# One kernel at its two ends: the order and norms of the first batch's scores, its first folds in single blocks, and the last short tile with its stores

## The chip, the cores and the metric

The kernel runs on one core of one Trainium2 chip. The metric is device time in microseconds (us) of one execution. The profile was taken from one execution of its own. Its engines are PE (TensorE), ACT (ScalarE), DVE (VectorE), POOL (GpSimd) and SP (SyncE); the latter two and ACT also issue DMA transfers.

## The reference

Four batches of 5824 tokens with 256 channels pass through an attention across channels, and the 23296 tokens that come out through a feed-forward part:

```python
qn = q / (np.linalg.norm(q, axis=1, keepdims=True) + 1e-06)
kn = k / (np.linalg.norm(k, axis=1, keepdims=True) + 1e-06)
s = kn.transpose(0, 2, 1) @ qn / tau          # 256 x 256 for each batch
s = s - s.max(-1, keepdims=True)
a = np.exp(s)
a /= a.sum(-1, keepdims=True) + 1e-09
x = (v @ a).reshape(B * S, D)
out = ((x @ w1) * (x @ w2) @ w3) @ w_out      # d_ff = 1024
```

The norms run over the tokens, so that each channel of q and of k has one. tau is 1.

## The kernel before

**What is folded.** The kernel never forms v @ a. For each batch it multiplies the softmax matrix into w1 and w2 (a *fold*; the result `Wf` has 256 rows and two times 1024 columns), and w3 into w_out once (`W_sb`, 1024 x 256). Each token then needs two products with `Wf` (a and b), their elementwise product, and one product with `W_sb`.

**Tiling.** A batch has 45 groups of 128 tokens (NT) and 64 more (LEFT). A token's row lies at partition p, slot i, so that partition p owns 45 neighbouring tokens; slots come in pieces of 8, the sixth piece having five, and its slot 5 (LAST) holds the 64 left rows with zeros below them. The feed-forward part takes chunks of four slots (512 tokens) and d_ff in eight blocks of 128. The 45th slot of a batch makes a *short* tile of 128 tokens, and with it, in every second batch, go the left rows of two batches, 2 x 64 = 128 tokens. For each chunk and block PE makes a and b in one PSUM bank each (`normal`, L979), ACT casts a to bf16 (L969), DVE multiplies (L1001), and later PE makes the output tile (`emit_out` L1111; others at L1073, and L814 in a form with seven products instead of eight, whose sums POOL makes). A planner with costs and due times orders this steady part, and the scores of later batches are put between its steps.

**The head.** Only the first batch's scores are laid out by hand, at L1205 to L1253. POOL issues the loads with a cast to bf16 (`load_part` L128): k and q by pieces, last k's piece 5, the rest of q's piece 4 (slots 4 and 5, then 6 and 7), q's piece 5 (left rows, slots 0 to 2, slots 3 and 4), then v and the weights. PE makes for every slot `products` (L287: q-transposed times k into the tile G, two matmuls of 256 columns) and `squares` (L275: a slot times itself into `sqq` or `sqk`, two matmuls of 128 columns, of which only the diagonal is wanted). Between these calls stand the steps of `soft_units(0)`, in the order of the program:

- `k_first` (L302): diagonal of k's squares, on DVE.
- `k_row` (L361): one fp32 matmul of PE, then four `root_step`s (L321: Ln, Exp of half, Ln of it plus 1e-6, Exp of minus) on ACT, which give 1/(norm + 1e-6), and DVE's transpose of it into the row `kr`.
- `q_first` (L380): DVE takes the diagonal of q's squares, in two halves `dq`, with the sum `ss`.
- `scaled_first` (L310): DVE makes s = G x kr in two halves (`scale`, L396); `q_norm` (L383) makes r = 1/(norm + 1e-6) with two ACT steps and two DVE steps; ACT makes e = exp(r x s) in two halves (`exps`, L401).
- `sum_start` (L405), then fillers: two 512-column matmuls on zeros (`busy(2)`), and the transposes of v's first four slots.
- `first_folds` (L510): for each half of e, PE's row sums (L421) and `narrow_fold(0, 128)`: columns 0 to 127 of w1 and of w2 side by side in one PSUM bank for each of the two channel halves c1. DVE takes the reciprocal of the sums (L429), and the evictions to `Wf` scale by it, c1 = 0 on ACT (L506), c1 = 1 on DVE (L508). Then the same for columns 128 to 255.

The first a of the steady part needs all of columns 0 to 127 of `Wf` for w1, and the first b those for w2.

**Buffers.** PSUM has eight banks, used by tag: ab0 to ab3, out0 to out2 and G. `bank("ab")` and `bank("out")` hand out the next of their tags in turn.

**The tail.** The last chunk of 512 tokens has its output in out0 and out1; ACT evicts the former (L1143), DVE the latter (L1144), and SP stores both. The last short tile (b = 3) has its 128 tokens in out0 and the left rows of batches 2 and 3 in out2. PE makes these 16 matmuls at the very end, beginning with one of the left rows and then one of the short tile. DVE evicts the left rows (L1126), ACT the short tile (L1137). SP stores the 64 rows of batch 2 (L1129), ACT's queue the short tile (L1139) and then the 64 rows of batch 3 (L1129). After batch 1 SP makes both stores of left rows.

Of the kernel before, what the change touches and what calls it, by code (L numbers as in the profile page):

```python
# [9 lines left out]
AF = mybir.ActivationFunctionType  # L10
ALU = mybir.AluOpType
F32 = DT.float32
BF16 = DT.bfloat16

P = 128
# [15 lines left out]
def kernel(  # L31
# [12 lines left out]
    nc = tc.nc  # L44
# [35 lines left out]
    def bank(tag):  # L80

        turns[tag] += 1
        return {"tag": f"{tag}{turns[tag] % (4 if tag == 'ab' else 3)}", "bufs": 1}
# [152 lines left out]
    def busy(k):  # L236

        m = psum.tile([P, 512], F32, name=f"warm_{nc.get_next_instruction_name()}", **bank("ab"))
        for _ in range(k):
            nc.tensor.matmul(m, lhsT=warm[:, :P], rhs=warm, start=True, stop=True, skip_group_check=True)  # L240
# [26 lines left out]
    def squares(nm, pi, slots, end=False):  # L267

        if nm not in S:
            S[nm] = psum.tile([P, CT, P], F32, name=f"sq{nm}_0", **bank("out"))  # L270
        t = pieces[nm, 0, pi]
        for i in slots:
            for ct in range(CT):
                cs = slice(ct * P, (ct + 1) * P)
                nc.tensor.matmul(  # L275
                    S[nm][:, ct, :], lhsT=t[:, i, cs], rhs=t[:, i, cs],
                    start=((pi, i) == ((4, half) if nm == "k" else (0, 0)) and ct == 0),
                    stop=(end and i == slots[-1] and ct == CT - 1), skip_group_check=True,
                )

    def products(pi, slots, end=False):
        if 0 not in G_tiles:
            G_tiles[0] = psum.tile([P, CT, C], F32, tag="G", name="G_0", bufs=1)
        qt, kt = pieces["q", 0, pi], pieces["k", 0, pi]
        for i in slots:
            for ct in range(CT):
                nc.tensor.matmul(  # L287
                    G_tiles[0][:, ct, :], lhsT=qt[:, i, ct * P : (ct + 1) * P], rhs=kt[:, i, :],
                    start=(pi == 0 and i == 0 and ct == 0),
                    stop=(end and i == slots[-1] and ct == CT - 1), skip_group_check=True,  # L290
                )

    def soft_units(n):
# [14 lines left out]
            nc.vector.tensor_add(st["ksq"], red[:, :8], st["kk"])  # L308

        def scaled_first():  # L310
            for ct in range(CT):
                scale(ct)
            q_norm(st["ss"])
            exps(0)
            exps(1)

        def partition_sums(dst, src):

            nc.vector.tensor_reduce(out=dst, in_=src, axis=mybir.AxisListType.X, op=ALU.add, apply_transpose=True)

        def root_step(t, i):  # L321

            nc.scalar.activation(
                out=t, in_=t, func=(AF.Ln, AF.Exp)[i % 2],
                scale=(1.0, 0.5, 1.0, -1.0)[i], bias=eps_t if i == 2 else 0.0,
            )

# [54 lines left out]

        def q_norm(src):  # L383
            r = work.tile([P, CT], F32, tag="r", name=f"r_{n}", bufs=2)
            nc.scalar.activation(out=r, in_=src, func=AF.Ln)
            nc.scalar.activation(out=r, in_=r, func=AF.Exp, scale=0.5)
            nc.vector.tensor_scalar_add(r, r, 1e-6)
            nc.vector.reciprocal(r, r)
            if inv_tau != 1.0:
                nc.vector.tensor_scalar_mul(r, r, inv_tau)  # L390
            st["r"] = r

        def scale(ct):
# [4 lines left out]
        def exps(ct):  # L398
            if ct == 0:
                st["e"] = work.tile([P, CT, C], BF16, tag="e", name=f"e_{n}", bufs=2)  # L400
            nc.scalar.activation(  # L401
                out=st["e"][:, ct, :], in_=st["s"][:, ct, :], func=AF.Exp, scale=st["r"][:, ct : ct + 1]
            )
# [88 lines left out]
        def narrow_fold(lo, hi, c1, c2):  # L492

            if c2 == 0:
                tag = "ab" if lo < 256 else "out"
                st[lo, c1] = psum.tile([P, 2, hi - lo], F32, name=f"narrow_{lo}_{c1}", **bank(tag))
            m = st[lo, c1]
            for w in range(2):
                nc.tensor.matmul(
                    m[:, w, :], lhsT=st["e"][:, c2, c1 * P : (c1 + 1) * P], rhs=w12[:, c2, w, lo:hi],  # L500
                    start=(c2 == 0 and w == 0), stop=(c2 == CT - 1 and w == 1), skip_group_check=True,
                )
            if c2 == CT - 1:
                dst = Wf[n][:, c1, :, lo:hi]
                if c1 == 0:
                    nc.scalar.activation(out=dst, in_=m, func=AF.Copy, scale=st["rs"][:, c1 : c1 + 1])  # L506
                else:
                    nc.vector.tensor_scalar_mul(dst, m, st["rs"][:, c1 : c1 + 1])  # L508

        def first_folds():  # L510
            for c2 in range(CT):
                sum_mm(c2)
                for c1 in range(CT):
                    narrow_fold(0, P, c1, c2)
            for c1 in range(CT):
                for c2 in range(CT):
                    narrow_fold(P, 2 * P, c1, c2)
# [169 lines left out]
        agenda.append((t, seq[0], cost, fn))  # L687

    out_tiles = {}
    last_rows = []  # L690
    lefts = {}

    def chunk_cols(c):
# [398 lines left out]
    def emit_out(b, c, j, ab, only=None):  # L1092

        small = c == NCH - 1
        if small:
            lhs = [ab[:, :P]]
            if b % 2 == 1:
                lhs.append(lefts[b // 2][:, j, :, :].rearrange("p b t -> p (b t)")[:, P : P + 2 * LEFT])
        else:
            lhs = [ab[:, i // 2, i % 2 * P : (i % 2 + 1) * P] for i in range(4)]  # L1100
        if j == 0:
            out_tiles[b, c] = [
                psum.tile([P, 2, D], F32, tag=tag, name=f"o_{b}_{c}_{tag}", bufs=1)
                for tag in ((("out0", "out2") if b == B - 1 else ("out0", "out1"))[: len(lhs)] if small else ("out0", "out1"))
            ]
        tl = out_tiles[b, c]
        for s, lhsT in reversed(list(enumerate(lhs))) if small and b == B - 1 else enumerate(lhs):
            if only is not None and s != only:
                continue
            h, o = (s, 0) if small else divmod(s, 2)  # L1110
            nc.tensor.matmul(  # L1111
                tl[h][:, o, :], lhsT=lhsT, rhs=W_sb[:, j, :],
                start=(j == 0 and o == 0), stop=(j == FT - 1 and (small or o == 1)),
                skip_group_check=True,
            )
        work_on("PE", len(lhs) * (D * MM_COL + MM_FIX))
        if j == FT - 1:
            read = now["PE"] + LATE["PE"]
            free["out0"] = work_on("ACT", 0.475, read)
            free["out1"] = work_on("DVE", 0.6, read)  # L1120
            o = work.tile([P, 4, D], F32, tag="o_sb", name=f"osb_{b}_{c}", bufs=3)
            rows = out[b * N : b * N + NT * P, :].rearrange("(p i) c -> p i c", i=NT)
            if small:
                if b % 2 == 1 and only != 0:
                    o2 = work.tile([P, D], F32, tag="kr", name=f"oleft_{b}", bufs=1)
                    nc.vector.tensor_copy(o2, tl[1][:, 0, :])  # L1126
                    for m in (b - 1, b):
                        k = (m - b + 1) * LEFT
                        store = lambda m=m, k=k, queue=nc.sync: queue.dma_start(  # L1129
                            out=out[m * N + NT * P : (m + 1) * N, :], in_=o2[k : k + LEFT, :]  # L1130
                        )
                        if m < B - 1:
                            store()
                        else:
                            last_rows.append(store)
                if only != 1:
                    nc.scalar.copy(o[:, 0, :], tl[0][:, 0, :])  # L1137
                    other = nc.scalar if b == B - 1 else nc.sync
                    other.dma_start(out=rows[:, NT - 1, :], in_=o[:, 0, :])  # L1139
                    if last_rows:  # L1140
                        last_rows.pop()(queue=nc.scalar)
            else:
                nc.scalar.copy(o[:, 0:2, :], tl[0])  # L1143
                nc.vector.tensor_copy(o[:, 2:4, :], tl[1])  # L1144
                nc.sync.dma_start(out=rows[:, 4 * c : 4 * c + 4, :], in_=o)
            if only is None:
                del out_tiles[b, c]
# [86 lines left out]
    squares("k", 4, hi)  # L1234
    squares("q", 4, lo)
    products(4, lo)
    squares("k", 5, range(LAST + 1), end=True)
    soft0[0]()
    for sl in (range(half, half + 2), range(half + 2, PIECE)):
        squares("q", 4, sl)  # L1240
        products(4, sl)
    soft0[1]()
    for sl in ([LAST, 0], [1, 2]):
        squares("q", 5, sl)
        products(5, sl)
    squares("q", 5, [3, 4], end=True)
    soft0[2]()
    products(5, [3, 4], end=True)
    soft0[3]()
    soft0[6]()  # L1250
    busy(2)
    transpose_half_on_pe(0, 0, 0, False)
    soft0[4]()  # L1253

# [234 lines left out]
```

## Time and profile before

| what | value |
|---|---|
| times of three runs | 552.27, 552.76, 553.76 us; median 552.76 |
| profiled execution | 552.28 us, of which the span 550.5 us |
| busy in the span | PE 539.2 us (98%), DVE 422.6 (77%), POOL 404.9 (74%), ACT 395.6 (72%) |
| TensorE clock granted | 1.00 |
| shares of the chain that ended last | PE 93%, DMA 5%, all others under 1% |

A line such as `L401 ACT e<-s,r` is a group of instructions made at line 401, on ACT, that write tile e from s and r. The *chain of waits* is followed back from the last instruction, at each step to what released it or to the one before it on its engine. *Waits* are idle times of an engine, put down to what ended them. In a *timeline* the first column is the start in the span, the second the length, and square brackets hold the idle time before and its releaser. *Landing* is the time from the issue of a DMA to its last byte.

### The profile page before, as it was taken

How to read it: one execution, taken by the hardware profiler on the slowest of the kernel's cores; microseconds unless marked ns; L12 is line 12 of the kernel's file. 1: busy time of each engine (PE TensorE's matmuls, PEld its weight loads, DVE VectorE, ACT ScalarE, POOL GpSimd, SP SyncE). 2: the span in 40 equal slices, each digit the busy share in tenths (PEclk: the TensorE clock that was granted, in tenths of full speed). 3: DMA queues.
4: the chain of work that ended last, by engine and by line, in shares of the span. 5: the costliest groups of instructions: out<-in, count | busy, mean ns of one | idle time of the engine just before them, and what ended most of it. 6: DMA issues, size and time to landing. Idle time of an engine off the chain costs nothing.

```text
span 550.5 us, 12142 instructions
## 1 busy us (share of the span) xinstructions
PE 539.2 (98%) x4563; PEld 350.9 (64%) x4563; DVE 422.6 (77%) x742; ACT 395.6 (72%) x813; POOL 404.9 (74%) x332
## 2 busy tenths in 40 slices
PE   7799999999999999999999999999999999999996
PEld 4564566666677666666658666666657656666675
DVE  5567749999876888888766788888777787878861
ACT  5446648889777888888666888888777767677662
POOL 4170398479899399799987598969998746889360
PEclk9999999999999999999999999999999999999999
DMA  9999987986685748975683857776661334750113
GB/s 214 212 204 208 210 168 163 208 166 129 130 187 113 187 88 165 181 167 110 136 162 110 168 120 153 160 144 109 144 128 78 84 86 109 151 95 39 78 44 129
DMA packets 75018, 77.58 MB, mean 141 GB/s; under 512 B 54224, under 2 KB 58832, under 8 KB 74960
## 3 DMA queue, kind: packets, MB, share of 16 engines
q0 software_dynamic: 15664, 38.93, 40.7%
q1 hardware_dynamic: 58928, 37.17, 24.7%
q10 hardware_dynamic: 368, 0.72, 0.4%
q8 instruction: 35, 0.57, 0.4%
q14 instruction: 23, 0.19, 0.1%
HBM read 78.91 MB, written 23.86 MB: 187 GB/s over the span
## 4 chain that ended last, share of the span: by engine, by line
PE 93%; DMA 5%; ACT 0%; POOL 0%; issue 0%; DVE 0%; ACTq 0%; POOLq 0%
PE a L979 26%; PE b L979 26%; PE prodA L814 12%; PE prodC L814 6%; PE G L214 5%; PE o L1073 4%; PE X L964 3%; PE prodB L814 3%; DMA k<-in_k_dram 3%; PE fold L450 2%; DMA q<-in_q_dram 2%; PE o_out L1111 2%; PE w L1258 1%; PE Z L964 1%; PE T L964 1%; PE Y L964 1%
## 5 line engine op out<-in xcount | busy, mean ns | idle before, releaser
L1001 DVE TENSOR_TENSOR abh<-as,b 128x512 bf16<-128x512 bf16 x314 | 214.0, 684 | 74.7 <-ACT as L969 53.6
L969 ACT CAST as<-a 128x512 bf16<-128x512 f32 (+1 forms) x346 | 194.4, 563 | 67.4 <-PE a L979 53.6
L979 PE MATMUL a<-vT,Wf 128*128 128x512 bf16 x628 | 186.8, 379 | 0.1
L979 PE MATMUL b<-vT,Wf 128*128 128x512 bf16 x628 | 186.8, 379 | 0.0
L979 PEld LDWEIGHTS <-Wf 128*128 128x128 bf16 x1384 | 124.9, 98 | 80.7 <-issue 0.3
L774 POOL TENSOR_TENSOR S<-abh,abh 128x1024 bf16<-128x1024 bf16 x37 | 78.8, 2130 | 62.5 <-DVE abh L1001 52.8
L228 DVE TENSOR_TENSOR acc<-acc,sq 128x512 f32<-128x512 f32 x132 | 91.6, 694 | 1.7 <-ACT sq L211 0.8
L814 PEld LDWEIGHTS <-S 128*128 128x128 bf16 x1184 | 77.8, 98 | 22.2 <-POOL S L776 0.5
L776 POOL TENSOR_TENSOR S<-S,abh 128x1024 bf16<-128x1024 bf16 x37 | 78.7, 2128 | 2.6
L776 POOL TENSOR_TENSOR S<-abh 128x1024 bf16<-128x1024 bf16 x37 | 79.2, 2142 | 0.1
L776 POOL TENSOR_TENSOR S<-abh,S 128x1024 bf16<-128x1024 bf16 x37 | 78.8, 2130 | 0.1
L814 PEld LDWEIGHTS <-abh 128*128 128x128 bf16 x888 | 58.8, 98 | 19.0 <-issue 0.3
L827 ACT COPY osb<-prodA 128x256 f32<-128x256 f32 x111 | 41.3, 372 | 18.3 <-PE prodA L814 18.1
L214 PE MATMUL G<-k,q 128*128 128x256 bf16 x276 | 52.3, 273 | 0.0
L214 PEld LDWEIGHTS <-q 128*128 128x128 bf16 x276 | 27.0, 98 | 32.1
L814 PE MATMUL prodA<-comb_T,S 128*128 128x128 bf16 x592 | 45.1, 219 | 0.0
L211 ACT ACTIVATE sq<-q 128x512 f32<-128x512 bf16 x69 | 43.8, 634 | 0.4 <-DVE acc L228 0.4
L211 ACT ACTIVATE sq<-k 128x512 f32<-128x512 bf16 x69 | 43.4, 629 | 0.0
L834 DVE TENSOR_TENSOR osb<-osb,prodC 128x256 f32<-128x256 f32 x74 | 30.6, 413 | 4.3 <-ACT osb L827 3.3
L1073 PE MATMUL o<-W_sb,abh 128*128 128x256 bf16 x192 | 27.0, 273 | 0.0
L128 POOL DMA_DIRECT2D q<-in_q_dram x27 | 15.1, 561 | 12.2 <-DMA q<-in_q_dram 5.7
L1073 PEld LDWEIGHTS <-abh 128*128 128x128 bf16 x192 | 18.7, 98 | 7.9
(160 smaller groups left out, 622.2 us busy)
## 6 DMA issues: line engine op xcount, KB each, us to landing
out_dram<-osb SPq DMA_DIRECT2D x44, 512.0 KB, 3.5
k<-in_k_dram POOLq DMA_DIRECT2D x19, 512.0 KB, 8.5
v<-in_v_dram POOLq DMA_DIRECT2D x19, 512.0 KB, 6.8
q<-in_q_dram POOLq DMA_DIRECT2D x18, 512.0 KB, 5.5
w<-in_moe_w_dram POOLq DMA_DIRECT2D x4, 512.0 KB, 16.9
k<-in_k_dram POOLq DMA_DIRECT2D x4, 320.0 KB, 7.9
v<-in_v_dram POOLq DMA_DIRECT2D x4, 320.0 KB, 4.5
q<-in_q_dram POOLq DMA_DIRECT2D x3, 320.0 KB, 5.8
```

What stands on the lines that cost most here:

```text
L211: nc.scalar.activation(out=sqs[0][:, :, part, :], in_=src[:, o : o + 2, :], func=AF.Square)
L214: nc.tensor.matmul(G[:, ct, :], lhsT=qt[:, i, ct * P : (ct + 1) * P], rhs=kt[:, i, :], start=(pr == 0 and part == 0 and ct == 0), stop=(pr ...
L228: nc.vector.tensor_add(accs[n], accs[n], sqs[0][:, part - 2])
L774: nc.gpsimd.tensor_add(x, a21, a22)
L776: nc.gpsimd.tensor_sub(x, *{2: (sums[1], a11), 3: (a11, a21)}.get(i) or (a12, sums[2]))
L814: nc.tensor.matmul(st[nm][:, i, :], lhsT=a[:, j, i * P : (i + 1) * P], rhs=w[j], start=(first and j == 0 and i == 0), stop=(j == 3), skip_ ...
L827: nc.scalar.copy(quarter(r, d), st[nm])
L964: nc.tensor.matmul(dst, lhsT=lhsT, rhs=rhs, start=start, stop=True, skip_group_check=True)
L969: nc.scalar.copy(a_sb[:, :n], t[:, :n])
L979: nc.tensor.matmul(t[:, :n], lhsT=Wf[b][:, ct, w, j * P : (j + 1) * P], rhs=rhs_of(b, c, ct), start=(ct == 0), stop=(ct == CT - 1),)
L1001: nc.vector.tensor_mul(ab, two_halves(a_sb), two_halves(t))
L1073: nc.tensor.matmul(t[:, k, :], lhsT=ab2[j // 4][:, h, j % 4, k * P : (k + 1) * P], rhs=W_sb[:, j, :], start=(j == 0 and k == 0), stop=(j = ...
```

## The change

- **Order.** k's piece 5 is squared with its left rows first. Of q's piece 5, all squares and only two slots' products stand ahead of `q_first`; before, four slots' products did. The other four slots' products follow it.
- **q's norm.** All four steps are `root_step`s on ACT, queued ahead of the two exps and in a tile that DVE doesn't touch; each exps follows its scale.
- **First folds.** Columns 0 to 127 are folded in four blocks (w, c1) of 128 x 128, each in its own ab bank with its own eviction, w1's first. Columns 128 to 255 take out banks instead of ab banks. `busy(2)` becomes `busy(1)`.
- **Tail.** The last short tile takes bank G instead of out0. The left rows of two batches go out in one store on SP, with the two batches as the outer dimension of the destination; ACT's queue no longer stores any.

```diff
         def scaled_first():
+            q_norm(st["ss"])
             for ct in range(CT):
                 scale(ct)
-            q_norm(st["ss"])
-            exps(0)
-            exps(1)
+                exps(ct)
...
-        def root_step(t, i):
+        def root_step(t, i, src=None):
 
             nc.scalar.activation(
-                out=t, in_=t, func=(AF.Ln, AF.Exp)[i % 2],
+                out=t, in_=t if src is None else src, func=(AF.Ln, AF.Exp)[i % 2],
                 scale=(1.0, 0.5, 1.0, -1.0)[i], bias=eps_t if i == 2 else 0.0,
             )
...
         def q_norm(src):
             r = work.tile([P, CT], F32, tag="r", name=f"r_{n}", bufs=2)
-            nc.scalar.activation(out=r, in_=src, func=AF.Ln)
-            nc.scalar.activation(out=r, in_=r, func=AF.Exp, scale=0.5)
-            nc.vector.tensor_scalar_add(r, r, 1e-6)
-            nc.vector.reciprocal(r, r)
+            for i in range(4):
+                root_step(r, i, src if i == 0 else r)
...
         def narrow_fold(lo, hi, c1, c2):
 
             if c2 == 0:
-                tag = "ab" if lo < 256 else "out"
-                st[lo, c1] = psum.tile([P, 2, hi - lo], F32, name=f"narrow_{lo}_{c1}", **bank(tag))
+                st[lo, c1] = psum.tile([P, 2, hi - lo], F32, name=f"narrow_{lo}_{c1}", **bank("out"))
...
+        def block_fold(w, c1, c2):
+
+            if c2 == 0:
+                st["block", w, c1] = psum.tile([P, P], F32, name=f"block_{w}_{c1}", tag=f"ab{2 * w + c1}", bufs=1)
+            m = st["block", w, c1]
+            nc.tensor.matmul(
+                m, lhsT=st["e"][:, c2, c1 * P : (c1 + 1) * P], rhs=w12[:, c2, w, :P], start=(c2 == 0), stop=(c2 == CT - 1)
+            )
+            if c2 == CT - 1:
+                dst = Wf[n][:, c1, w, :P]
+                if c1 == 0:
+                    nc.scalar.activation(out=dst, in_=m, func=AF.Copy, scale=st["rs"][:, c1 : c1 + 1])
+                else:
+                    nc.vector.tensor_scalar_mul(dst, m, st["rs"][:, c1 : c1 + 1])
+
         def first_folds():
             for c2 in range(CT):
                 sum_mm(c2)
                 for c1 in range(CT):
-                    narrow_fold(0, P, c1, c2)
+                    block_fold(0, c1, c2)
+            for c1 in range(CT):
+                for c2 in range(CT):
+                    block_fold(1, c1, c2)
...
-                for tag in ((("out0", "out2") if b == B - 1 else ("out0", "out1"))[: len(lhs)] if small else ("out0", "out1"))
+                for tag in ((("G", "out2") if b == B - 1 else ("out0", "out1"))[: len(lhs)] if small else ("out0", "out1"))
...
-                    for m in (b - 1, b):
-                        k = (m - b + 1) * LEFT
-                        store = lambda m=m, k=k, queue=nc.sync: queue.dma_start(
-                            out=out[m * N + NT * P : (m + 1) * N, :], in_=o2[k : k + LEFT, :]
-                        )
-                        if m < B - 1:
-                            store()
-                        else:
-                            last_rows.append(store)
+                    nc.sync.dma_start(
+                        out=out.rearrange("(m n) d -> m n d", n=N)[b - 1 : b + 1, NT * P :, :], in_=o2
+                    )
...
-                    if last_rows:
-                        last_rows.pop()(queue=nc.scalar)
...
-    squares("k", 5, range(LAST + 1), end=True)
+    squares("k", 5, [LAST])
+    squares("k", 5, range(LAST), end=True)
     soft0[0]()
     for sl in (range(half, half + 2), range(half + 2, PIECE)):
         squares("q", 4, sl)
         products(4, sl)
     soft0[1]()
-    for sl in ([LAST, 0], [1, 2]):
-        squares("q", 5, sl)
-        products(5, sl)
+    squares("q", 5, [LAST])
+    products(5, [LAST])
+    squares("q", 5, [0, 1, 2])
+    products(5, [0])
     squares("q", 5, [3, 4], end=True)
     soft0[2]()
-    products(5, [3, 4], end=True)
+    products(5, [1, 2, 3, 4], end=True)
     soft0[3]()
     soft0[6]()
-    busy(2)
+    busy(1)
     transpose_half_on_pe(0, 0, 0, False)
     soft0[4]()
```

## The prediction

> **What bounds the kernel now.** I read the page's chain first, then PE's waits, then the chain's two ends, and last the tail's timeline and landings.
>
> ```profile
> PE 93%; DMA 5%; ACT 0%; POOL 0%; issue 0%; DVE 0%; ACTq 0%; POOLq 0%
> ```
>
> From 40 us to 537.9 us the chain has PE steps alone. All of PE's waits in the run:
>
> ```profile
> PE sqq L275 <- DMA q<-in_q_dram: 4.5, 4, 1.7
> PE warm_I-94_95 L246 <- DVE ones_pp L92: 1.4, 1, 1.4
> PE sum L421 <- ACT e L401: 0.4, 1, 0.4
> PE o_out L1111 <- ACT osb L1143: 0.3, 1, 0.3
> PE sqk L275 <- DMA k<-in_k_dram: 0.2, 1, 0.2
> ```
>
> (total us, times, longest). Only o_out's lies behind 40 us. PE's work between the ends stays, so the ends add to the time one for one. The head's chain (start, length, step):
>
> ```profile
> 32.35 0.44 PE G L287 x4
> 32.78 0.24 PE sqq L275 x4
> 33.02 0.02 issue
> 33.05 0.04 DVE dq L374
> ...
> 34.24 0.09 DVE r L387
> 34.33 0.02 issue
> 34.35 0.17 DVE r L388
> 34.52 0.02 issue
> 34.55 0.52 ACT e L401
> ...
> 36.02 0.48 ACT Wf L506
> 36.50 0.05 issue
> 36.54 0.60 PE a L979 x2
> ```
>
> PE reaches q's last squares behind products that nobody awaits yet; e waits for r; a waits for the first Wf. The tail, as timeline:
>
> ```profile
> 544.63 1.80 PE L1111 MATMUL o_out<-W_sb,left 128*128 128x256 bf16 x15 [0.34 <-ACT osb L1143]
> ...
> 546.70 0.49 SPq L1129 DMA_DIRECT2D out_dram<-oleft  x1
> 546.91 0.36 ACTq L1139 DMA_DIRECT2D out_dram<-osb  x1
> 547.31 0.64 ACTq L1129 DMA_DIRECT2D out_dram<-oleft  x1
> ```
>
> and the times from issue to landing there:
>
> ```profile
> out_dram<-osb ACTq DMA_DIRECT2D x1, 128.0 KB, 2.5
> out_dram<-oleft SPq DMA_DIRECT2D x1, 64.0 KB, 2.3
> out_dram<-oleft ACTq DMA_DIRECT2D x1, 64.0 KB, 2.2
> ```
>
> The last landing is 547.31 + 2.2 = 549.5, and the span ends 1.0 later, at 550.5.
>
> **What the Trainium skill says.** *DMA: Bandwidth & Descriptors*, section "Why a DMA increments its semaphore by 16 and not by 1": a transfer runs on the largest number k of engines, at most 16, that divides the slowest dimension above size 1 of both patterns. Old left stores: 64 rows against 64 partitions, k = 16. New one: two batches of 64 rows against 128 partitions, k = 2. The trace of before agrees for 16 (queue records of the old stores show their rows spread and done in about 0.8 us) and has no store with a small outer dimension. *ScalarE: Activation LUTs*, section "What ACT_TABLE_LOAD costs": a per-partition pointer operand adds about 93 ns to an ACTIVATE. The trace agrees: the k row's steps take 0.16 us, the one with eps_t 0.24. *TensorE: Matmul & The Clock Gate*, section "Architectural detail", has ACT and DVE run their queues strictly in order; the trace shows k_row's ACT and DVE steps in program order.
>
> **The change, part by part.**
>
> *k's left rows first.* Two matmuls move into PE's wait for k's piece 5. At most 2 x 0.056 = 0.11; the next q load lands only at 15.64 + 14.0 = 29.64, and PE follows q's loads from there. Counted at 0; range 0 to 0.11 gained.
>
> *Order of q's last piece.* Four matmuls of 256 columns leave the stretch before the last squares: 4 x 0.109 = 0.44. The squares' start (timeline) moves from 32.62 to 32.18, just after their data (issued 26.28, landed 5.8 later: 32.08). DVE's dq is then bounded not by them but by kr, which DVE makes in order before it (32.29, 0.45 long; consecutive DVE steps overlap by 0.08): 32.66 in place of 33.05, a gain of **0.39**. The delayed products end at 33.02 - 0.44 + 8 x 0.109 = 33.45 at most; s follows at 33.45 to 33.48, as before, and its second half is done near 34.2.
>
> *q's norm on ACT.* ss is read by 33.16, Ln starts at 33.20. Steps in SBUF: the Ln at 33.59 and the Exp at 33.83 are 0.24 apart; with the eps operand 0.24 + 0.08 = 0.32. So 0.24 + 0.24 + 0.32 + 0.24 = 1.04, e starts at 34.24. Before it was 0.96 from Ln to e: the norm is 0.08 slower, and together with the order e gains 0.39 - 0.08 = **0.31**. What ACT's queue holds behind the norm is the exps, which wait for it anyway; s waits on neither. The first s is ready at 33.45 + 0.42 = 33.87 and covers nothing of this, but it would be late next if r came over 0.37 sooner; exps by halves costs nothing.
>
> *Folds in blocks.* Sums and reciprocal follow e: 0.31 earlier, ACT's first eviction starts near 35.71. The matmuls stay 16. An eviction of 128 x 128 isn't in the trace: ACT takes 0.47 for 256 and 0.69 for 512 columns, the line through them gives 0.36 for 128; DVE (0.48, 0.75) 0.35. Bounds 0.30 to 0.47. ACT's block ends at 36.07, DVE's near 36.08, a starts near 36.11 in place of 36.54: **0.43** gained. w2's blocks end near 36.44, when b needs them at 36.54. Range of the head 0.25 to 0.6: if blocks cost 0.47 or the last squares' data came late, the gain falls to the former. Columns 128 to 255 in out banks have 0.2 us or more to spare.
>
> *busy(1).* It takes 0.22 of PE filler away; PE idled before the sums. The wait for e grows by 0.22 - 0.31, so shrinks. Cost 0.
>
> *Bank G.* PE's second matmul at the end waits for ACT to empty out0 (544.12 to 544.63). G was read last by DVE's left products, long before. **0.51** gained for PE, and for the evictions and issues: SP's left store at 546.19, ACT's at 546.40.
>
> *One left store.* The old one has its first row 1.46 us after its issue; a 1 KB row takes an engine 46 ns (median of the tail's ACT queue records). On two engines each gets 64 rows and 8 of the short tile's: 72 x 0.046 = 3.31. Landing: 546.19 + 1.46 + 3.31 = 550.96, against 549.51 before. So the tail, bank G included, costs **1.45**. ACT's last issue (0.64) goes, unseen. SP's queue holds nothing behind this store. After batch 1 (issued 322.9) only the short tile's store is behind it, and the source buffer's next use is batch 3's kr at 400.2: cost 0.
>
> The sum: -0.43 + 1.45 = +1.02. The profiled execution becomes 552.28 + 1.02 = 553.30; the median of the runs shown stood 0.48 above it, so **553.8**.
>
> **The rivals.** A measurement of this kernel tells about 0.3%, 1.66 us, from no change; my forecast is inside that.
>
> *The store spreads over 16 engines after all.* For it: no run here shows k = 2, and descriptors may be regrouped on the way to the queue. Then 8 rows each, and the last to land is the short tile, 546.40 + 2.5 = 548.9, 0.6 before the old end. Sum -0.43 - 0.6 = -1.03: 551.7 (551.1 to 552.3).
>
> *Slower: two engines do rows slower than 46 ns.* In the tail, SP's old rows took 77 ns (median) when both queues were busy. Then 72 x 0.077 = 5.54, landing 553.19, tail +3.68, sum +3.25: 556.0. It decides from 1.66 + 0.43 = 2.09 of tail, which is (2.09 + 3.31 - 1.45)/72 = 55 ns per row. Against it: no second queue has work then, save 128 rows spread wide.
>
> *The head doesn't gain.* The squares' data has 0.1 us of cover; a load landing 0.5 later, or eviction blocks bound by something fixed, would eat the 0.43. With the store as forecast: 554.2. In the chain of before, POOL's loads set the pace up to 32 us, which speaks for it a little.
>
> **How the numbers follow.** Store on two engines, head as worked out: 0.58, 553.8, its own range 553.1 to 554.6. Spread: 0.30. Slow rows: 0.07. No head gain: 0.05. The forecast is the likeliest. The range reaches down to most of the spread case and up over the row price's small excesses: 551.3 to 555.0, leaving out some 0.07 below and 0.08 above. Faster by over 0.3% (under 551.1) needs the spread case at its lowest: 0.07. Slower (over 554.4): the slow rows, 0.07, a tenth of the forecast's case and a third of the last, 0.15 together. The rest, 0.78, is the same.
>
> **What would show it.** SP's left store lands 4.5 to 5 us after its issue (spread: about 2.5), and is the last to land. e starts near 34.2, a near 36.1, with ACT's r steps four and DVE's none. PE's wait for osb is gone. The span is about 551.5. It would be wrong if the store's landing stayed under 3 us, if a started after 36.4, or if a new PE wait showed behind 40 us.

## The result and the profile after

| | before | after |
|---|---|---|
| median of 7 runs | 552.71 us (552.27 to 553.76) | 554.46 us (554.24 to 555.0) |
| profiled execution | 552.28, span 550.5 | 554.24, span 552.5 |

The ratio is 1.0032, with a 95% interval of 1.0020 to 1.0044: 1.75 us slower, against a forecast of 1.1 (553.8 against 552.71) and a range up to 555.0.

The page's chain, then all of PE's waits, in the changed kernel:

```profile
PE 92%; DMA 5%; ACT 1%; DVE 0%; POOL 0%; issue 0%; ACTq 0%; POOLq 0%
```

```profile
PE sqq L275 <- DMA q<-in_q_dram: 4.2, 3, 1.7
PE warm_I-94_95 L246 <- DVE ones_pp L92: 1.4, 1, 1.4
PE sqq L275 <- ACT q L1184: 0.6, 1, 0.6
PE sum L418 <- ACT e L398: 0.2, 1, 0.2
```

The wait for ACT's eviction at the tail is gone, as is half of the wait for e. The head's part of the chain of waits (start, length, step):

```profile
32.23 0.45 DVE kr L345
32.68 0.06 DVE dq L373
...
33.11 0.02 issue
33.14 0.21 ACT r L322
33.35 0.02 issue
33.37 0.21 ACT r L322
33.58 0.02 issue
33.61 0.30 ACT r L322
33.91 0.02 issue
33.93 0.21 ACT r L322
34.15 0.02 issue
34.17 0.92 ACT e L398 x2
...
35.69 0.45 PE narrow L495 x8
36.14 0.53 PE a L992 x2
```

kr now stands in the chain, as the bound of dq, and four ACT steps lead to e at 34.17. The chain leads to a through PE's own folds, since PE is hardly idle there; the timeline of ACT and of PE has a at 36.06, and 0.05 before it the end of ACT's first block eviction (two evictions on the first line, the first from 35.64 to 36.01):

```profile
35.64 0.62 ACT L517 ACTIVATE Wf<-block,rs 128x128 bf16<-128x128 f32 x2 [0.56 <-PE block L511]
36.06 0.60 PE L992 MATMUL a<-vT,Wf 128*128 128x512 bf16 x2
```

So the eviction still stands right ahead of a, as before (36.49 and 36.54), and is shorter. kr's own start differs from profile to profile, 32.21 to 32.53 among the fourteen, so the head is best counted from it: from kr to a 3.83 us in place of 4.25, 0.42 gained. The head does what was forecast. The tail, as timeline:

```profile
545.46 0.42 DVE L1139 COPY oleft<-o_out 128x256 f32<-128x256 f32 x1 [0.84 <-PE o_out L1124]
545.72 0.37 ACT L1144 COPY osb<-o_G 128x256 f32<-128x256 f32 x1 [1.43 <-PE o_G L1124]
545.91 0.57 SPq L1140 DMA_DIRECT2D out_dram<-oleft  x1
546.12 0.35 ACTq L1146 DMA_DIRECT2D out_dram<-osb  x1
```

SP issues the left store 0.79 earlier than before, and still the end is 2.0 later. The DMA view from 545 to 553 us, in 40 slices of 0.2 us (mean busy share of the 16 engines in tenths; GB/s), shows why:

```profile
DMA  0049899990037964322211101111100000000000
GB/s 0 0 205 410 348 492 389 410 369 0 20 77 179 277 118 72 56 41 41 41 36 36 31 26 36 51 51 51 36 26 10 0 0 0 0 0 0 0 0 0
```

First the last full chunk at 350 to 490 GB/s, then the last two stores: a peak, and 3 us of a trickle at 26 to 56 GB/s. The queue records have the left store's 128 rows on SP's queue, with two closing records of 4 bytes, where each old store has 16. The rows take 3.99 us from first to last. The DMA view has no landing of this store, but its semaphore has its last two updates at 551.09 and 551.44, so it landed at 551.44; ACT's short tile did at 549.6. Before, the last landing was at 549.5.

### The profile page after: what moved, and what is told of

It reads as the page before. It is cut to its first block, busy times and chain, and to the rows that moved or that the text cites. A ratio compares the mean times of both kernels' runs of the same rounds, so it can differ in the third digit from the quotient of the medians.

```text
span 552.5 us, 12140 instructions
## 1 busy us (share of the span) xinstructions
PE 538.7 (97%) x4562; PEld 350.7 (63%) x4562; DVE 421.2 (76%) x741; ACT 395.9 (72%) x816; POOL 404.5 (73%) x332
## 4 chain that ended last, share of the span: by engine, by line
PE 92%; DMA 5%; ACT 1%; DVE 0%; POOL 0%; issue 0%; ACTq 0%; POOLq 0%
PE a L992 26%; PE b L992 25%; PE prodA L827 12%; PE prodC L827 6%; PE G L214 5%; PE o L1086 4%; PE X L977 3%; PE prodB L827 3%; DMA k<-in_k_dram 3%; PE fold L447 2%; DMA q<-in_q_dram 2%; PE o_out L1124 1%; PE w L1265 1%; PE Y L977 1%; PE T L977 1%; PE Z L977 1%
```

## The experiments

All times are medians, each group beside its own runs of the kernel before (552.4).

**Is it the store?** The changed kernel with the old stores (shown), and the kernel before with the new one (the same lines the other way round):

```diff
-                    nc.sync.dma_start(
-                        out=out.rearrange("(m n) d -> m n d", n=N)[b - 1 : b + 1, NT * P :, :], in_=o2
-                    )
+                    for m in (b - 1, b):
+                        k = (m - b + 1) * LEFT
+                        store = lambda m=m, k=k, queue=nc.sync: queue.dma_start(
+                            out=out[m * N + NT * P : (m + 1) * N, :], in_=o2[k : k + LEFT, :]
+                        )
+                        if m < B - 1:
+                            store()
+                        else:
+                            last_rows.append(store)
...
+                    if last_rows:
+                        last_rows.pop()(queue=nc.scalar)
```

> The changed kernel with the two old left stores (SP's and ACT's), all else as changed. Theory (two engines carry the one store, and this is the whole loss): the last landing is ACT's left store, issued near 546.5, landing 2.2 later, 548.7; the span ends 1.0 to 1.45 later, 549.7 to 550.2; time about 551.5 to 552.0, faster than the kernel before by 0.7 to 1.2 us. Rival (the loss lies elsewhere, in PE's stretch between the ends or in the end of the run): about 553.5 to 554, still slower than before.

Measured: 551.55 against 552.39 (ratio 0.9992, 0.9979 to 1.0005, one of its 14 runs being 5 us longer than the rest). The profile ends at 549.9.

> The kernel before with only the one left store. Theory: issued at 546.7 as before, it lands 5.1 later (as in the changed kernel), 551.8, the only store behind all others; span 552.8 to 553.3, so 2.3 to 2.8 us slower than before. Rival (store harmless, the loss lies in the other edits): within 0.5 us of before.

Measured: 555.30 against 552.39, ratio 1.0050 (1.0038 to 1.0062). In both directions the store costs 2.6 to 2.9 us: 555.30 - 552.39 = 2.9 in the kernel before; in the changed kernel 1.75 + 0.84 = 2.6, each time taken against its own runs of the kernel before (554.46 - 551.55 = 2.9 without that). The upper end of what was expected of the second is passed because the store lands 5.5 us after its issue there (552.45 - 546.93), as in the changed kernel (551.44 - 545.91), and not 5.1. The rival falls: all of the loss is the store's, and the rest of the change, taken together, gains (the interval here touches 1; that of the version with both left stores on SP, below, doesn't).

The same store stands after batch 1, too, and costs nothing there: PE's steps in the changed kernel are 0.47 ahead of those in the kernel before both ahead of it (b at 299.46 for 299.93) and behind it (a at 366.35 for 366.82). Only as the last store does it cost.

**Is it the number of engines?** The same single store of 128 rows with other outer dimensions. Both kernels put left rows where they don't belong in the output, and serve for the times alone:

```diff
-                        out=out.rearrange("(m n) d -> m n d", n=N)[b - 1 : b + 1, NT * P :, :], in_=o2
+                        out=out.rearrange("(m n) d -> n m d", n=N)[NT * P :, b - 1 : b + 1, :], in_=o2
```

> The changed kernel with the dimensions of its one left store swapped: 64 rows outside, the two batches inside, so that left rows land in permuted places (the left rows of the output are permuted). Theory (k is the largest number up to 16 that divides both outer dimensions, here 16): lands 2.2 to 2.5 after its issue near 545.9, so 548.3, and the last landing is ACT's short tile near 548.6 to 549.6; time 551.3 to 552.3. Rival (two batches in one pattern are slow for another reason, such as row pitch in DRAM): lands 5 us after its issue, 554.4.

Measured: 551.44 against 552.39, ratio 0.9983 (0.9976 to 0.9991). Its landings, and the DMA view from 545 to 553 us:

```profile
out_dram<-oleft SPq DMA_DIRECT2D x1, 128.0 KB, 2.1
out_dram<-osb ACTq DMA_DIRECT2D x1, 128.0 KB, 2.3
```

```profile
DMA  0000000798989504999300000000000000000000
GB/s 0 0 0 0 0 0 0 307 451 369 451 369 451 225 0 154 348 328 364 118 0 0 0 0 0 0 0 0 0 0 0 0 0 0 0 0 0 0 0 0
```

(This execution's tail lies 1 us later than the changed kernel's; the shape counts.) The trickle is gone: the rows take 0.53 us, all 16 engines close the store, and it lands 2.1 after its issue.

```diff
-                        out=out.rearrange("(m n) d -> m n d", n=N)[b - 1 : b + 1, NT * P :, :], in_=o2
+                        out=out.rearrange("(m n) d -> m n d", n=N)[0:4, NT * P : NT * P + LEFT // 2, :], in_=o2
```

> The changed kernel with its one left store written as 4 batches of 32 rows, so that left rows land in wrong batches and half of the left rows' places get other rows or none. Theory: k = 4, so 32 rows on each engine: 1.15 + (32 + 8) x 0.046 to 0.062, so 3.0 to 3.6 us to the landing, near 549.2; time about 552.2 to 552.8, half way between 16 and 2 engines. Rival (all or nothing, not the number of engines): 554.4 or 551.5.

Measured: 552.84 against 552.39, ratio 1.0009 (1.0001 to 1.0016). Four closing records, and 2.34 us of rows. The DMA view from 545 to 553 us lies between the two others, with a trickle of 72 to 138 GB/s:

```profile
DMA  0000099999930378553322220000000000000000
GB/s 0 0 0 0 0 451 389 410 389 451 389 144 0 87 200 225 138 128 97 82 72 72 97 97 15 0 0 0 0 0 0 0 0 0 0 0 0 0 0 0
```

The same bytes in one store on the same queue take 3.99, 2.34 and 0.53 us with an outer dimension of 2, 4 and 64. This is what the Trainium skill says in *DMA: Bandwidth & Descriptors*, section "Why a DMA increments its semaphore by 16 and not by 1" (engines: the largest number up to 16 that divides both slowest dimensions), and the closing records, 2, 4 and 16, agree with it one for one.

**Why 3.99 and not 3.31?** Without the short tile's store:

```diff
-                    other = nc.scalar if b == B - 1 else nc.sync
-                    other.dma_start(out=rows[:, NT - 1, :], in_=o[:, 0, :])
+                    if b < B - 1:
+                        nc.sync.dma_start(out=rows[:, NT - 1, :], in_=o[:, 0, :])
```

> The changed kernel without the last short tile's store (its 128 rows of batch 3 are left out of the output), so that the two-engine store runs alone. In the changed kernel its rows take 3.99 us, 62 ns apart, with gaps, where 64 rows of 46 ns would be 2.9. Theory (the short tile's rows that run at the same time hold it up): the rows take 2.7 to 3.0 us, the last landing comes 1.0 to 1.2 earlier, time about 553.3. Rival (two engines just do rows at 62 ns): 3.9 to 4.0 us, 554.4.

Measured: 553.75 against 552.40, ratio 1.0026 (1.0016 to 1.0035), rows in 3.32 us. Neither theory had its number. The short tile's eight rows on each engine cost 0.67, not the 0.37 of their own records; but alone, too, 64 rows take 52 ns each, not 46, as some records are longer (6 of 128 over 100 ns). What lengthens those stays open.

**A second way to store.** Against the changed kernel with two left stores:

```diff
+                        store()
-                        if m < B - 1:
-                            store()
-                        else:
-                            last_rows.append(store)
```

> The changed kernel with two left stores of 64 rows, both issued by SP. Expected: SP issues the second 0.5 after the first, near 546.5, landing 2.2 later, with ACT's short tile about the same; time 551.3 to 551.6, equal to or 0.1 to 0.2 under the version with the second on ACT's queue.

Measured: 551.59 against 552.40, ratio 0.9986 (0.9979 to 0.9993), the same as with the second store on ACT's queue (551.55).

**The bank alone.**

```diff
-                for tag in ((("out0", "out2") if b == B - 1 else ("out0", "out1"))[: len(lhs)] if small else ("out0", "out1"))
+                for tag in ((("G", "out2") if b == B - 1 else ("out0", "out1"))[: len(lhs)] if small else ("out0", "out1"))
```

> The kernel before with bank G for the last short tile and nothing else. Theory: PE's wait for ACT's eviction (0.5 us with the step) goes, all later issues and landings move with it: 0.5 us faster than before. Rival (the last landing is held by the queue of stores ahead, not by PE): within 0.1.

Measured: 551.93 against 552.40, 0.47 faster, ratio 0.9993 (0.9985 to 1.0002). The size is the theory's; the interval touches 1. In the profiles SP's left store comes 0.50 earlier against PE's steps ahead of the tail.

**The head alone.** All edits of the head and none of the tail; the edit is the diff of the change without its parts `out_tiles` and stores.

> The kernel before with all edits of the head and none of the tail. Theory: the first a starts 0.40 earlier, as in the changed kernel, and the end moves with it: 0.3 to 0.45 us faster than before. Rival (given back in the steady part): a starts 0.40 earlier, time within 0.1 of before.

Measured: 552.40 against 552.40, ratio 0.9999 (0.9990 to 1.0007). The times leave open whether the head gains: this interval holds everything from 0.55 faster to 0.39 slower, while the two-store kernel, which has the head and the bank, stands 0.38 below the bank alone (551.55 and 551.93). The profiles tell more. From kr to a this one has 3.83 us, as the changed kernel has: 0.42 gained. It keeps 0.39 of it up to 519 us. Then comes DVE's multiply at 519.65, which DVE could have started at 519.27, and PE's next step on a buffer of the same chain is late. The timeline of this kernel for DVE, and for PE:

```profile
518.62 0.70 DVE L1049 TENSOR_TENSOR Z<-X,t 128x512 f32<-128x512 f32 x1
519.65 0.69 DVE L1015 TENSOR_TENSOR abh<-as,b 128x512 bf16<-128x512 bf16 x1 [0.33 <-ACT as L983]
```

```profile
520.32 0.59 PE L993 MATMUL b<-vT,Wf 128*128 128x512 bf16 x2
520.99 0.38 PE L978 MATMUL X<-tsum,Wf 128*128 128x512 bf16 x1
```

The same pair of PE in the kernel before starts 0.43 apart (520.73, 521.16), here 0.67. The release that the trace names, an ACT cast, isn't one that this multiply waits for: in the timeline of the test below it starts at 519.18, while that cast runs until 519.55. The same multiply is late in all seven kernels here with all of the head's edits (the test below apart), and on time in all those without. In the listing of DVE's instructions (waits included) it is number 1216 = 19 x 64 with the edits, which take one away, and 1217 without. Two more multiplies that turned late, at 198 and 306 us, are numbers 448 and 704, both multiples of 64; one that was late before and is on time now, at 360, was number 832 = 13 x 64 and is 831. So a test:

```diff
+    pad = consts.tile([P, 1], F32)
+    nc.vector.memset(pad, 0.0)
     ones_f = consts.tile([P, 1], F32)
```

> The changed kernel with two left stores, and one more DVE instruction at the very start (a memset of an unused tile). In the runs with the head's edits DVE's multiply at 519.7 starts 0.37 late and PE then waits 0.22; it is DVE's instruction number 1216 = 19 x 64 there, and number 1217 in the kernel before, where it is on time. Theory (DVE stalls at each 64th instruction of its stream, which hurts where that instruction is awaited): with one more instruction it is number 1217 again, the 0.22 come back, time 0.2 below the version without the extra memset, about 551.35. Rival (the late multiply has to do with the earlier start or the banks): it stays late, time equal or later.

Measured: 551.44 against 552.42, ratio 0.9981 (0.9973 to 0.9989). The timelines of DVE (with the cast on ACT) and PE:

```profile
518.52 0.70 DVE L1051 TENSOR_TENSOR Z<-X,t 128x512 f32<-128x512 f32 x1
518.92 0.63 ACT L985 CAST as<-Y 128x512 bf16<-128x512 f32 x1
519.18 0.69 DVE L1017 TENSOR_TENSOR abh<-as,b 128x512 bf16<-128x512 bf16 x1
```

```profile
520.22 0.59 PE L995 MATMUL b<-vT,Wf 128*128 128x512 bf16 x2
520.65 0.38 PE L980 MATMUL X<-tsum,Wf 128*128 128x512 bf16 x1
```

One memset at the start, and 519 us later the multiply is on time and PE's pair 0.43 apart. All three late multiplies (198, 306 and 519 us) are on time; the one at 360 is number 832 again and late again, as in the kernel before, and PE's lead over that kernel is 0.50 ahead of it and behind it. In the profile the 0.2 came back; of the time, 0.11 between medians of different groups is too little to call shown. That the stall goes with the instruction's number is shown; what makes it isn't.

The DVE streams of all fourteen profiles narrow it down. An instruction with nothing more to wait for starts about 0.045 us after the end of the wait (an instruction of its own) ahead of it. In one run or another, numbers 192, 448, 576, 704, 832, 960, 1088 and 1216 stand right behind such a wait, and there each starts 0.39 us after it at the earliest, mostly 0.40; all are odd multiples of 64. The even ones show nothing: 768 (in seven runs) and 1152 (in five) start 0.045 after their waits, and 128, 640 and 1024 start just as the same instructions do with another number. So, as far as these streams show, the stall comes once in 128 instructions, and is seen only where no longer wait and no running instruction covers it.

**The head's parts, one at a time.** First the order of q's last piece:

```diff
-    for sl in ([LAST, 0], [1, 2]):
-        squares("q", 5, sl)
-        products(5, sl)
+    squares("q", 5, [LAST])
+    products(5, [LAST])
+    squares("q", 5, [0, 1, 2])
+    products(5, [0])
     squares("q", 5, [3, 4], end=True)
     soft0[2]()
-    products(5, [3, 4], end=True)
+    products(5, [1, 2, 3, 4], end=True)
```

> The kernel before with only the new order of q's last piece (last squares ahead of four more slots' products). Theory: kr-bound squares, so e and the first a start 0.39 earlier against kr, and since no instruction is added or taken on any engine, all of it arrives at the end: 0.3 to 0.4 us faster. Rival (given back because the steady part absorbs an earlier start): first a earlier, time within 0.1 of before.

Measured: 552.36 against 552.42, ratio 0.9997 (0.9988 to 1.0005). From kr to a 4.20 in place of 4.25: both theories are wrong. The timeline of DVE says why:

```profile
33.20 0.08 DVE L374 DVE_READ_ACCUMULATOR2_ANT ss<- 128x1 f32 x1
33.57 0.76 DVE L396 TENSOR_TENSOR s<-G,kr 128x256 f32<-128x256 f32 x2 [0.29 <-PE G L287]
34.24 0.16 DVE L387 TENSOR_SCALAR r<-r 128x2 f32<-128x2 f32 x1
34.44 0.17 DVE L388 RECIPROCAL r<-r 128x2 f32<-128x2 f32 x1
```

ss is ready early, as forecast, and ACT's two steps are done by 33.8. But r's two DVE steps are queued behind s, and s waits for G, which comes no sooner.

> The kernel before with only q's norm on ACT. Theory by the sum: four ACT steps take 1.04 us from Ln to e where two ACT and two DVE steps took 0.96, so e and a start 0.08 later. Rival (two crossings between engines cost more than the trace's steps show): e earlier than before.

The edit is that of `scaled_first`, `root_step` and `q_norm` in the change. Measured: 552.42 against 552.42, ratio 1.0000 (0.9992 to 1.0008). kr to e 2.33 in place of 2.26, kr to a 0.08 more: as the theory has it, though too small for the times.

> The kernel before with only the first folds in 128 x 128 blocks. Theory: the eviction ahead of a takes 0.36 in place of 0.47, so from e to a 1.87 in place of 1.99, 0.12 less; the time 0.1 less. Rival (evictions of 128 columns cost as much as of 256): no change from e to a.

The edit is that of `narrow_fold`, `block_fold` and `first_folds`. Measured: 552.66 against 552.42, ratio 1.0003 (0.9995 to 1.0011). From e to a 1.89 in place of 1.99, near the theory's 0.12; it doesn't arrive in the time. DVE's stream has one more instruction here than before, number 1216 is the Z two ahead of the multiply, and from there on PE's steps in this profile are a further 0.28 behind (0.13 before, 0.41 after).

## Why the prediction was right, and where its sizes were off

The likeliest case was the right one, with a loss larger than its sum. The median is 0.66 above the forecast, the profiled execution 0.94 (554.24 for 553.30); the difference is luck, since the 0.48 that was added for the median was 0.22 this time. Step by step, in the profiled executions:

- *The store on two engines*: right, the sign and the cause. Its sum gave the last landing at 550.96 - 0.43 = 550.53; it was 551.44. Of the 0.91 between, the rows are 0.68 (3.99 for 3.31), the time outside the rows 0.08 (1.54 for 1.46), and SP's issue 0.15 (545.91 for 545.76). (The 1.46 isn't the time to the first row, as the prediction has it, but the old store's 2.3 to landing less 0.84 of rows; its first row comes 1.14 after the issue, here 1.21, and the rest lies between the last row and the landing. The sum holds.) The mis-sized term is "72 x 0.046": the records' median taken as the pace of a whole queue. With 3.99 it is 55 ns per row (3.99 / 72), which is the very point that the slower rival named for 0.3%, and the result lies there.
- *Spread over 16 engines*: fell. A store that did spread gives 551.44, where this rival had 551.7.
- *Bank G*: 0.47 measured for 0.51.
- *The head*: from kr, a comes 0.42 earlier for 0.43, and blocks and norm have their sizes (0.10 for 0.11 to 0.12; 0.08 for 0.08). But the split was wrong: "a gain of 0.39" for the order needs the norm on ACT, since else r's DVE steps stand behind s. Alone the order is worth 0.05, the norm -0.08; together 0.32 (kr to e 1.94 for 2.26). The sum held because the change makes both.
- *"The ends add to the time one for one"*: failed by 0.2 for the head. PE's work between the ends stayed, and yet a multiply of DVE at 519 us came late, because the change took one instruction from DVE's stream. PE's lead in the changed kernel falls there from 0.48 to 0.26, and this is the 0.15 at SP's issue, less some hundredths by which a came earlier than forecast in this profile. "No head gain", the last rival, named other causes than this.
- *k's left rows first*, counted at 0: no run has it alone. kr starts at 32.21 to 32.45 in the eight profiles with it and at 32.29 to 32.53 in the six without; what it is worth stays open.

Best of those tried: the changed kernel with two left stores and the padding memset, 551.44, 0.98 us faster than before and 2.7 faster than the change as it was made (0.98 + 1.75).

## What to carry to other kernels

One store in place of two saves an issue, and can take the engines away that carry it: look at what the outermost dimension becomes, and above all at the last store, which nothing hides. Where a step is freed on one engine, ask which queue its result passes next; two edits can each be worth next to nothing (0.05 and -0.08 here) and together 0.3. And a gain at one end is proved at the other end only: follow it through the trace by the same instruction in both kernels.

## What was not expected of the hardware

- DVE starts some instructions late, by 0.10 to 0.38 us, whose number in its stream is an odd multiple of 64 (192, 448, 704, 832 and 1216 among them); where another wait or a running instruction covers it, nothing is seen. Adding or taking a single instruction moves them, and with them 0.2 us of this kernel's profile.
- Rows of 1 KB on two engines: 52 ns each alone (3.32 / 64), and eight rows of another store on each of these engines cost 84 ns each (0.67 / 8), though the median record is 46 ns long.
